# Value matmuls in the banks of the transpositions, four kinds of copies on ScalarE, and weight conversions directly behind the maxima, in a fused attention and gated-convolution kernel

## The chip, the cores and the metric

The kernel runs on one core of a Trainium2 chip. The metric is the time of one execution on the device in microseconds, the median of several runs.

## The reference

Attention with rotary positions over 4 batches, 8 heads, 576 positions and a head size of 64, followed by a block with two projections (512 to 1024 and back) around a convolution of width 3 and a gate. All is float32; the weights of the second half come as 64-bit floats.

```python
q_rot, k_rot = (rotate(q), rotate(k))
scores = scale * np.matmul(q_rot, k_rot.transpose(0, 1, 3, 2))
scores = scores - np.max(scores, axis=-1, keepdims=True)
attn = np.exp(scores)
attn = attn / (np.sum(attn, axis=-1, keepdims=True) + 1e-09)
attn_out = np.matmul(attn, v)
x = attn_out.transpose(0, 2, 1, 3).reshape(B, S, H * D)
h = np.maximum(x @ w_in, 0.0)
conv_out = sum(conv_w[k] * hp[:, k:k + S, :] for k in range(3))   # hp: h, padded
gate = 1.0 / (1.0 + np.exp(-conv_out))
return h * gate @ w_out
```

## The kernel before

**Attention.** Two heads make a pair, and there are 16 pairs `p`. A pair takes five slots of a list that is written out by hand (`plan`): slot 5p+s handles the query rows of step `s`, 128 rows for s = 0 to 3 and the 64 remaining rows of both heads for s = 4. The steps of a pair and their names below are:

- `emit_TQ(p, "q" / "r" / "k")`, lines 175 and 185: the rotated q, the remainders and the rotated k are transposed on TensorE into a bank of PSUM and copied to `QT` and `KT`. They stand in slots 5p-4, 5p-3 and 5p-2.
- `emit_S`, line 206: the scores, in a bank of the pool `s`. Then VectorE takes the maxima (`reds`, line 214), and ScalarE the exponentials with their sums (`exps`, line 218).
- `emit_T` and `emit_Trem`, lines 263, 275 and 280: the exponentials are transposed, and copied to `PT` (line 162 on ScalarE, line 164 on VectorE).
- `emit_E(p, 0)` in slot 5p+4 and `emit_E(p, 1)` in slot 5p+5, line 316: the products with v ("the v matmuls" below, the first and the second of a pair), each of 290 columns; ScalarE copies the result to `xn` (line 324).
- `emit_rinv` and `emit_rinvT`, lines 289 to 304: the reciprocals of the sums are transposed, copied to `rst` (line 297), and spread over the partitions by two DMAs on SP's queue; `norm` (line 328) multiplies `xn` with them two slots later, and `split` (line 332 on ScalarE, 333 on GpSimd) cuts the product into a high and a low part.

**The other half.** From slot 24 on (`WIDE`), `emit_M1` (line 347, in twelve matmuls, evacuated by ScalarE's relu in line 355, then convolution, tanh and gate) and `emit_M2` (line 425, four quarters of six matmuls that keep one bank of PSUM open until the last) are put between the attention's steps. Ten slots are one block: eight of them have an `emit_M1`, the first has several quarters of `emit_M2`. Before slot 24 the weights are converted from 64-bit floats in 48 steps, about two to a slot: `first` (ScalarE, line 443), `mid` (three instructions of VectorE, lines 446, 452 and 455) and `third` (VectorE, line 460; it also issues the load of a later piece and, two ticks later, ScalarE's and GpSimd's `split`, lines 503 and 504).

**Banks.** Before slot 24 the pool `s` has two buffers of three banks, and the pool `t` two banks for all else. From slot 24 on, `s` has two buffers of two banks, `t` two banks for the transpositions, and `m` two banks for `emit_M1`, `emit_M2` and the v matmuls. After the attention there is one pool of six banks.

**Order.** Every engine runs its instructions in the order in which they are emitted. In a slot that order goes by rank: before slot 24, transpositions of the slot before (0), maxima (0.2), exponentials (0.3), a conversion step (0.4), the scores of the next slot (0.5), `emit_rinv` and `norm` (1.7), q/k and remainder transpositions and `emit_rinvT` (2), a second conversion step (3), v matmuls (4). From slot 24 on: scores (0), maxima (0.2), transpositions (1), exponentials (1.5), then 1.7, 2 and 4, with the units of the other half spread between the ranks 2 and 4. A tick follows each event of the ranks 0, 0.5, 1, 2 and 4, and work that was deferred by some ticks is emitted there.

Of the kernel before, what the change touches and what calls it, by code (L numbers as in the profile page):

```python
# [20 lines left out]
def attention_moe_kernel(ctx, tc, q, k, v, w_in, conv_w, w_out, tab, out):  # L21
    nc = tc.nc
    B, H, S, D = q.shape
# [11 lines left out]
    scale = float(D) ** -0.5  # L35
# [4 lines left out]
    psum = {}  # L40
# [35 lines left out]
    def defer(k, fn, rank=1):  # L76
        due.setdefault(slot[0] + k, []).append((rank, len(due.get(slot[0] + k, [])), fn))
# [6 lines left out]
    def t_tile():  # L84
        return psum["t"].tile([128, 512], F32, tag="t", name="tp")

    def m_tile():
        if late["tail"]:
            return psum["t"].tile([128, 512], F32, tag="mt", name="mt")
        return psum["m"].tile([128, 512], F32, tag="m", name="pm")  # L90
# [67 lines left out]
    QT, KT = {}, {}  # L158

    def evac(eng, out, in_, sc=None):  # L160
        if eng == "A" or "m" not in psum:
            nc.scalar.activation(out=out, in_=in_, func=AF.Copy, scale=1.0 if sc is None else sc)  # L162
        elif sc is None:
            nc.vector.tensor_copy(out, in_)
        else:
            nc.vector.tensor_scalar(out=out, in0=in_, scalar1=sc, scalar2=None, op0=ALU.mult)

    def emit_TQ(p, part):
        if p not in QT:
            QT[p] = p2.tile([128, S], F32, tag="qT", name="qT")  # L170
            KT[p] = p2.tile([128, S + 64], F32, tag="kT", name="kT")
        ps = t_tile()
        t1 = rot.pop((p, part)).rearrange("p n d -> p (n d)")
        if part == "r":
            nc.tensor.transpose(ps[:, 0:128], t1, idf)
            evac("V", QT[p][:, 512:S], ps[:, 0:64], scale)
            evac("V", KT[p][:, 576:640], ps[:, 64:128])
            evac("V", KT[p][:, 0:64], ps[:, 64:128])
            if p * STEPS < WIDE:
                for h in range(2):  # L180
                    r = slice(64 * h, 64 * h + 64)
                    evac("V", krem[p % 2][r, r], ps[r, 64:128])
        else:
            for t in range(4):
                nc.tensor.transpose(ps[:, 128 * t:128 * t + 128], t1[:, 128 * t:128 * t + 128], idf)  # L185
            if part == "q":
                evac("A", QT[p][:, 0:512], ps, scale)
            else:
                evac("V", KT[p][:, 64:576], ps)

    ST, STR, PT = {}, {}, {}
    negm, sums = {}, {}
# [99 lines left out]
    def emit_rinvT(p):  # L292
        s = p % 2
        ps = t_tile()[0:32, 0:128]
        nc.tensor.transpose(ps, rvc[s], idf)
        st = p1.tile([32, 128], F32, tag="rst", name="rst")
        nc.vector.tensor_copy(st, ps)
        d = scr.tile([9, 128], F32, tag="d", name="rd")
        nc.sync.dma_start(out=d, in_=st[0:9, :])
        fl = d.rearrange("(o t) n -> o (t n)", o=1)  # L300
        rbt = rb[p] = p1.tile([128, S], F32, tag="rb", name="rb")
        nc.sync.dma_start(out=rbt[0:64, :], in_=fl[:, 0:S].to_broadcast([64, S]))
        nc.sync.dma_start(out=rbt[64:128, 0:512], in_=fl[:, 640:1152].to_broadcast([64, 512]))
        nc.sync.dma_start(out=rbt[64:128, 512:S], in_=fl[:, 576:640].to_broadcast([64, 64]))
# [4 lines left out]

    def emit_E(p, j):  # L310
        b, hp = divmod(p, NPB)
        xp = m_tile() if "m" in psum else t_tile()
        o = (S - XW) * j
        for i in range(5):
            for h in range(2):
                nc.tensor.matmul(  # L316
                    out=xp[64 * h:64 * h + 64, 0:XW],
                    lhsT=vmain[p][:, h, i, :] if i < 4 else vrem[p % 2][:, h, :],
                    rhs=PT[p][:, 2 * i + h if i < 4 else 8, o:o + XW],
                    start=(i == 0),  # L320
                    stop=(i == 4),
                )
        xn = p2.tile([128, XW], F32, tag="xn", name="xn", bufs=3)
        nc.scalar.activation(out=xn, in_=xp[:, 0:XW], func=AF.Copy)  # L324

        def norm():
            sl = xslot[b, hp, j] = free_slots.pop(0)
            nc.vector.tensor_tensor(out=xn, in0=xn, in1=rb[p][:, o:o + XW], op=ALU.mult)  # L328

        def split():  # L330
            sl = xslot[b, hp, j]
            nc.scalar.activation(out=xT[:, sl, 0, :], in_=xn, func=AF.Copy)  # L332
            nc.gpsimd.tensor_tensor(out=xT[:, sl, 1, :], in0=xn, in1=xT[:, sl, 0, :].bitcast(F32), op=ALU.subtract)  # L333

        norms[p, j] = lambda: (norm(), defer(1, split))
# [205 lines left out]
    plan = {}  # L541
# [3 lines left out]
    def at(n, rank, fn):  # L545
        plan.setdefault(n, []).append((rank, len(plan.get(n, [])), fn))

    def emit():
        with tc.manual_schedule(engines=engines):
# [6 lines left out]
            for part in "qrk":  # L556
                emit_TQ(0, part)
# [7 lines left out]
            for p in range(1, NP):  # L565
                n = STEPS * p
                if p > 1:
                    at(max(n - 9, 0), 19, lambda p=p: load(p))
                at(max(n - 8, 0), 18, lambda p=p: rope(p, "q", nc.gpsimd))
                at(max(n - 6, 0), 18, lambda p=p: rope(p, "r", nc.gpsimd))  # L570
                at(max(n - 6, 0), 18, lambda p=p: rope(p, "k", nc.gpsimd))
                for e, part in ((4, "q"), (3, "r"), (2, "k")):
                    at(n - e, 2, lambda p=p, part=part: emit_TQ(p, part))
                at(n, 19, lambda p=p: load_v(p))
            for p in range(NP):
                n = STEPS * p
                for s in range(STEPS):
                    m = n + s
                    first = m < WIDE
                    if m:  # L580
                        at(m - 1 if first else m, 0.5 if first else 0, lambda p=p, s=s: emit_S(p, s))
                    at(m, 0.2, lambda p=p, s=s: go(reds, (p, s)))
                    at(m, 0.3 if first else 1.5, lambda p=p, s=s: go(exps, (p, s)))
                    for h in range(2 if s < 4 else 1):
                        at(m + 1, 0 if m + 1 < WIDE else 1, lambda p=p, s=s, h=h: emit_T(p, s, h))
                for g, e in ((0, 2), (1, 4), (2, 5)):
                    at(n + e, 2, lambda p=p, g=g: emit_Trem(p, g))
                at(n + 4, 4, lambda p=p: emit_E(p, 0))
                at(n + 5, 4, lambda p=p: emit_E(p, 1))
                at(n + 5, 1.7, lambda p=p: emit_rinv(p))  # L590
                at(n + 6, 2, lambda p=p: emit_rinvT(p))
                for j in range(2):
                    at(n + 8, 1.7 + j, lambda p=p, j=j: norms.pop((p, j))())
            nw = len(wsteps)
            for i, u in enumerate(wsteps):
                x = (WIDE - 1) * i // nw
                at(x, 0.4 if not any(r == 0.4 for r, _, _ in plan.get(x, [])) else 3, u)
            at(12, 3, conv_cw)
            at(14, 2, turn_cw)
            moe = {}  # L600
# [61 lines left out]
            for u in seq + second + m2_units(last) + m2_units(LASTB):  # L662
                u()
                tick()

    emit()


# [41 lines left out]
```

## Time and profile before

| | |
|---|---|
| median of 3 runs | 579.53 us (578.71 to 579.86) |
| the profiled execution: time, span | 579.58 us, 577.5 us |
| TensorE (PE) busy | 522.2 us, 90% of the span |
| VectorE (DVE) busy | 382.1 us, 66% |
| ScalarE (ACT) busy | 315.3 us, 55% |
| GpSimd (POOL) busy | 270.7 us, 47% |
| granted clock of TensorE, mean | 0.979 |

The span runs from the first to the last instruction; 2.08 us of the profiled execution's time lie outside it. The span falls in three stages: attention with the conversion of weights (slots 0 to 23, to about 131 us), attention with the other half between it (to about 505 us), and the rest of the other half. Busy shares are averages over these.

### The profile page before, as it was taken

How to read it: one execution, taken by the hardware profiler on the slowest of the kernel's cores; microseconds unless marked ns; L12 is line 12 of the kernel's file. 1: busy time of each engine (PE TensorE's matmuls, PEld its weight loads, DVE VectorE, ACT ScalarE, POOL GpSimd, SP SyncE). 2: the span in 40 equal slices, each digit the busy share in tenths (PEclk: the TensorE clock that was granted, in tenths of full speed). 3: DMA queues.
4: the chain of work that ended last, by engine and by line, in shares of the span. 5: the costliest groups of instructions: out<-in, count | busy, mean ns of one | idle time of the engine just before them, and what ended most of it. 6: DMA issues, size and time to landing. Idle time of an engine off the chain costs nothing.

```text
span 577.5 us, 9313 instructions
## 1 busy us (share of the span) xinstructions
PE 522.2 (90%) x3297; PEld 374.5 (65%) x3297; DVE 382.1 (66%) x671; ACT 315.3 (55%) x821; POOL 270.7 (47%) x341
## 2 busy tenths in 40 slices
PE   3797968889998998999899998999989999989997
PEld 1354544446866685767657676767857677669986
DVE  4776987984888277655858458653776547457971
ACT  2677886885857265645627355652636537224530
POOL 5555948768375438190733629181281203132440
PEclk9989989899999999999989999999989999999999
DMA  6434343521302120201303121021200010010011
GB/s 182 123 108 116 114 135 99 151 61 23 83 2 63 39 75 10 66 15 40 81 1 82 40 60 24 30 51 58 64 22 20 20 40 21 2 58 18 1 37 54
DMA packets 67537, 33.07 MB, mean 57 GB/s; under 512 B 60412, under 2 KB 61220, under 8 KB 67492
## 3 DMA queue, kind: packets, MB, share of 16 engines
q1 hardware_dynamic: 66292, 32.10, 20.2%
q8 instruction: 26, 0.43, 0.3%
q10 hardware_dynamic: 1200, 0.39, 0.3%
q14 instruction: 19, 0.16, 0.1%
HBM read 27.68 MB, written 4.79 MB: 56 GB/s over the span
## 4 chain that ended last, share of the span: by engine, by line
PE 69%; DVE 13%; ACT 11%; issue 4%; DMA 2%; SPq 1%; ACTq 0%; DVEq 0%
PE sp L206 13%; PE pm L316 11%; PE pm L425 10%; PE tp L263 9%; PE pm L347 8%; PE mt L425 6%; PE mt L347 4%; ACT st L218 4%; PE tp L316 4%; DVE negm L214 3%; DVE c L361 3%; ACT pt L162 2%; PE tp L185 2%; DVE xn L328 1%; DVE c L359 1%
## 5 line engine op out<-in xcount | busy, mean ns | idle before, releaser
L379 POOL TENSOR_TENSOR g<-c,g 128x288 fp32r<-128x288 f32 (+4 forms) x88 | 56.0, 648 | 214.7 <-ACT g L378 213.0
L162 ACT ACTIVATE pt<-tp 128x512 f32<-128x512 f32 (+2 forms) x161 | 88.0, 565 | 101.7 <-PE tp L263 99.5
L214 DVE TENSOR_REDUCE negm<-sp 128x1 f32<-128x576 f32 x144 | 102.5, 748 | 51.6 <-PE sp L206 51.5
L206 PE MATMUL sp<-kT,qT 64*128 64x288 f32 (+4 forms) x560 | 109.7, 481 | 5.3 <-ACT st L218 5.2
L218 ACT ACTIVATE st<-sp,negm 128x576 f32<-128x576 f32 x128 | 93.7, 744 | 11.1 <-DVE negm L214 11.0
L263 PE MATMUL tp<-tabs,st 128*128 128x128 f32 x512 | 75.3, 289 | 18.5 <-ACT kr L162 6.8
L361 DVE SCALAR_TENSOR_TENSOR c<-rr,cw,c 128x288 f32<-128x288 f32 x128 | 88.0, 688 | 4.5
L263 PEld LDWEIGHTS tp<-tabs,st 128*128 128x128 f32 x512 | 57.5, 146 | 45.7 <-issue 13.0
L347 PE MATMUL pm<-xT,winh 128*128 128x290 f32 x384 | 82.9, 308 | 0.6 <-ACT xn L324 0.6
L206 PEld LDWEIGHTS sp<-kT,qT 64*128 64x128 f32 (+1 forms) x560 | 49.1, 180 | 40.9 <-issue 15.9
L316 PE MATMUL pm<-pt,vm 128*64 128x290 f32 x384 | 54.9, 430 | 12.7 <-ACT rr L355 12.7
L425 PE MATMUL pm<-wouth,g 128*128 128x512 f32 x176 | 64.3, 415 | 0.0
L347 PEld LDWEIGHTS pm<-xT,winh 128*128 128x128 f32 x384 | 61.1, 190 | 1.2 <-ACT xn L324 1.1
L347 PE MATMUL pm<-xT,winl 128*128 128x290 f32 x192 | 56.9, 296 | 0.0
L370 DVE SCALAR_TENSOR_TENSOR c<-c,rr 128x288 f32<-128x288 f32 x64 | 38.8, 607 | 16.3 <-ACT c L367 16.2
L316 PEld LDWEIGHTS pm<-pt,vm 128*64 128x64 f32 x384 | 26.4, 141 | 34.0 <-ACT rr L355 15.0
L324 ACT ACTIVATE xn<-pm 128x290 f32<-128x290 f32 x24 | 9.9, 413 | 63.3 <-PE pm L316 62.9
L425 PEld LDWEIGHTS pm<-wouth,g 128*128 128x128 f32 x176 | 33.2, 188 | 13.4 <-issue 7.0
L359 DVE TENSOR_SCALAR c<-rr,cw 128x288 f32<-128x288 f32 x64 | 31.4, 491 | 9.1 <-ACT rr L355 8.6
L347 PEld LDWEIGHTS pm<-xT,winl 128*128 128x128 f32 x192 | 36.6, 191 | 0.0
L425 PE MATMUL pm<-woutl,g 128*128 128x512 f32 x88 | 34.7, 395 | 0.0
L333 POOL TENSOR_TENSOR xT<-xn,xT 128x290 fp32r<-128x290 f32 x32 | 29.2, 925 | 11.0 <-ACT xT L332 11.0
(103 smaller groups left out, 881.8 us busy)
## 6 DMA issues: line engine op xcount, KB each, us to landing
out<-ot SPq DMA_DIRECT2D x17, 256.0 KB
rk<-k SPq DMA_DIRECT2D x32, 128.0 KB
w<-moe_w_in SPq DMA_DIRECT2D x8, 512.0 KB
vm<-v SPq DMA_DIRECT2D x32, 128.0 KB
w<-moe_w_out SPq DMA_DIRECT2D x8, 512.0 KB
rq<-q SPq DMA_DIRECT2D x30, 128.0 KB
rb<-rd SPq DMA_DIRECT2D x16, 144.0 KB
rb<-rd SPq DMA_DIRECT2D x16, 128.0 KB
```

Of the source, the lines that this page charges most:

```text
L162: nc.scalar.activation(out=out, in_=in_, func=AF.Copy, scale=1.0 if sc is None else sc)
L206: nc.tensor.matmul(out=out, lhsT=qt[64 * h:64 * h + 64, c], rhs=kt[64 * h:64 * h + 64, a:a + n], start=True, stop=True)
L214: reds.setdefault((p, s), []).append(lambda: nc.vector.tensor_reduce(out=nm, in_=sc, axis=AX.XY if len(sc.shape) == 3 else AX.X, op=ALU.ma ...
L218: lambda: nc.scalar.activation(out=dst, in_=sc, func=AF.Exp, bias=nm, scale=1.0, accum_out=sm)
L263: nc.tensor.transpose(ps[:, 128 * t:128 * t + 128], st[:, 128 * t:128 * t + 128], idf)
L316: nc.tensor.matmul(out=xp[64 * h:64 * h + 64, 0:XW], lhsT=vmain[p][:, h, i, :] if i < 4 else vrem[p % 2][:, h, :], rhs=PT[p][:, 2 * i + h ...
L347: nc.tensor.matmul(out=ps[:, 0:XW], lhsT=w[:, kk, fs], rhs=xT[:, xs, e, :], start=(i == 0), stop=(i == n - 1))
L359: nc.vector.tensor_scalar(out=c, in0=r[:, j:j + HS], scalar1=cw[:, f:f + 1], scalar2=None, op0=ALU.mult)
L361: nc.vector.scalar_tensor_tensor(out=c, in0=r[:, j + e:j + e + HS], scalar=cw[:, 8 * e + f:8 * e + f + 1], in1=c, op0=ALU.mult, op1=ALU.add,)
L370: nc.vector.scalar_tensor_tensor(out=c, in0=c, scalar=1.0, in1=r[:, j + 1:j + 1 + HS], op0=ALU.add, op1=ALU.mult)
L379: nc.gpsimd.tensor_tensor(out=lo, in0=c[:, o:o + n], in1=hi.bitcast(F32), op=ALU.subtract)
L425: nc.tensor.matmul(out=ops[tt][:, 0:width], lhsT=g_tile(tt, f, e), rhs=w[:, f, cols], start=(f == 0 and i == 0), stop=(f == NF - 1 and i = ...
```

## The change

The v matmuls always take a bank of the pool `t`. The copies of the transposed remainders (to `QT` and twice to `KT`) and of the transposed k go to ScalarE in all slots; before slot 24 they were there already, since `evac` uses ScalarE wherever there is no pool `m`. For the same reason the copy of the transposed reciprocals, now an `evac("V", ...)`, moves to ScalarE before slot 24 and stays on VectorE after it. All conversion steps get rank 0.4, so that both of a slot stand behind its maxima and exponentials and ahead of everything else.

```diff
         if part == "r":
             nc.tensor.transpose(ps[:, 0:128], t1, idf)
-            evac("V", QT[p][:, 512:S], ps[:, 0:64], scale)
-            evac("V", KT[p][:, 576:640], ps[:, 64:128])
-            evac("V", KT[p][:, 0:64], ps[:, 64:128])
+            evac("A", QT[p][:, 512:S], ps[:, 0:64], scale)
+            evac("A", KT[p][:, 576:640], ps[:, 64:128])
+            evac("A", KT[p][:, 0:64], ps[:, 64:128])
...
             else:
-                evac("V", KT[p][:, 64:576], ps)
+                evac("A", KT[p][:, 64:576], ps)
...
         st = p1.tile([32, 128], F32, tag="rst", name="rst")
-        nc.vector.tensor_copy(st, ps)
+        evac("V", st, ps)
...
-        xp = m_tile() if "m" in psum else t_tile()
+        xp = t_tile()
...
                 x = (WIDE - 1) * i // nw
-                at(x, 0.4 if not any(r == 0.4 for r, _, _ in plan.get(x, [])) else 3, u)
+                at(x, 0.4, u)
```

## Rows read from the trace of the kernel before

**Rows 1.** Busy time, granted clock and DMA in two stages, by windows.

```profile
14.00:131.00 117.00, 97.58 (x562) 53.86 (x558) 93.79 (x134) 90.38 (x228) 77.90 (x82) 0.93 0.41 113
131.00:505.00 374.00, 353.43 (x2336) 258.88 (x2335) 236.65 (x439) 198.82 (x520) 164.94 (x218) 0.99 0.15 39
```

**Rows 2.** Waits of TensorE, whole span: us in total, times, longest.

```profile
PE pm L316 <- ACT rr L355: 12.7, 10, 2.4
...
PE tp L263 <- ACT kr L162: 6.8, 4, 2.2
...
PE tp L263 <- DVE rst L297: 1.8, 4, 0.5
...
PE pm L347 <- ACT xn L324: 0.6, 1, 0.6
PE tp L316 <- DVE cw L525: 0.5, 1, 0.5
```

**Rows 3.** Timeline around one pair of v matmuls: start, duration, instruction, idle before.

```profile
219.22 0.59 ACT L162 ACTIVATE pt<-tp 128x512 f32<-128x512 f32 x1
...
220.22 0.38 PE L275 MATMUL tp<-tabs,st 128*128 128x128 f32 x2
...
221.32 0.74 ACT L218 ACTIVATE str<-sp,negm 128x576 f32<-128x576 f32 x1 [1.51 <-DVE negm L214]
...
222.05 0.40 ACT L355 ACTIVATE rr<-pm 128x289 f32<-128x289 f32 x1
...
222.51 2.17 PE L316 MATMUL pm<-pt,vm 128*64 128x290 f32 x16 [1.91 <-ACT rr L355]
...
231.29 2.17 PE L316 MATMUL pm<-pt,vm 128*64 128x290 f32 x16 [0.95 <-ACT rr L355]
```

**Rows 4.** The same work after three of these waits, by windows.

```profile
222.50:225.20 2.70, 2.69 (x21) 1.45 (x21) 2.35 (x3) 0.29 (x1) 2.62 (x4) 1.00 0.00 0
...
288.00:292.30 4.30, 4.15 (x21) 1.92 (x21) 3.77 (x4) 0.43 (x2) 4.00 (x4) 0.64 0.01 4
...
425.50:430.00 4.50, 4.43 (x21) 2.21 (x22) 4.05 (x4) 0.35 (x3) 4.34 (x6) 0.62 0.00 0
```

**Rows 5.** Groups by form: copies of k and of remainders (count, busy us, mean ns, idle before).

```profile
L164 DVE COPY kT<-tp 128x512 f32<-128x512 f32 x10 | 6.8, 680 | 0.4 <-PE tp L185 0.4
...
L162 ACT ACTIVATE kT<-tp 128x512 f32<-128x512 f32 x6 | 3.6, 604 | 0.6 <-PE tp L185 0.6
...
L162 ACT ACTIVATE kT<-tp 128x64 f32<-128x64 f32 x12 | 2.1, 234 | 0.0
```

**Rows 6.** Timeline, first stage, of slots 6, 7, 11, 13, 14 and 17.

```profile
48.41 0.28 DVE L297 COPY rst<-tp 32x128 f32<-32x128 f32 x1 [4.70 <-PE tp L295]
...
48.84 0.63 PE L263 MATMUL tp<-tabs,st 128*128 128x128 f32 x4 [0.46 <-DVE rst L297]
...
49.44 0.60 ACT L162 ACTIVATE qT<-tp 128x512 f32<-128x512 f32 x1
...
51.03 1.42 DVE L214 TENSOR_REDUCE negm<-sp 128x1 f32<-128x576 f32 x2
...
52.48 0.74 ACT L218 ACTIVATE st<-sp,negm 128x576 f32<-128x576 f32 x1 [1.09 <-DVE negm L214]
...
73.74 0.67 ACT L443 ACTIVATE wt<-w 128x512 f32<-128x512 f32 x1 [0.80 <-DVE wf L460]
...
83.56 1.64 DVE L455 SCALAR_TENSOR_TENSOR wt<-w,wt 128x512 int32<-128x512 int32 x1
...
84.54 0.46 ACT L332 ACTIVATE xT<-xn 128x290 fp32r<-128x290 f32 x1
...
101.82 0.74 ACT L218 ACTIVATE st<-sp,negm 128x576 f32<-128x576 f32 x1 [0.90 <-DVE negm L214]
```

**Rows 7.** Timeline, second stage, behind a transposition of remainders at 243.33 us.

```profile
244.50 0.56 ACT L378 ACTIVATE g<-c 128x224 fp32r<-128x224 f32 x2
...
245.55 1.09 PE L263 MATMUL tp<-tabs,st 128*128 128x128 f32 x8
```

## Prediction

> **What bounds the kernel now.** I read the windows by stage first, then TensorE's waits, then the timeline where the longest of them stand. Over the second stage TensorE is busy 353.4 of 374.0 us, VectorE 236.7 and ScalarE 198.8; in the first stage three engines stand close together, at 97.6, 93.8 and 90.4 of 117.0 us [rows 1]. So the second stage is TensorE's, and a microsecond that TensorE idles there is lost; the first is a chain through three engines, in which moving work from one to another can give or cost.
>
> The longest wait of TensorE is the v matmuls' for ScalarE's relu (line 355): 12.7 us in 10 places [rows 2]. The timeline shows its nature. The transposition of line 275 ends at 220.60; the v matmuls start at 222.51, just behind the relu that ends at 222.45 [rows 3]. No data goes from that relu to the v matmuls. What they share is the pool `m`: one bank holds an open sum of `emit_M2`, the other held the `emit_M1` before, and the relu empties it. The relu is late because ScalarE's queue stood 1.51 us at an exponential that waited for VectorE's maxima [rows 3]. One slot later, at 231.29, the second v product of the pair pays 0.95 us in the same way [rows 3]; five pairs have such a couple.
>
> **Part by part: the v matmuls' bank.** The wait for the relu goes: -12.7 us. The 0.6 us that an `emit_M1` waits for `xn`, the copy of a v product in its bank, goes too [rows 2]. What is late next? The new bank was last used by the second transposition of the slot, whose copy ends at 219.81, 0.79 us ahead of 220.60 [rows 3]. If a copy of k at 0.60 us [rows 5] slips ahead of it, 0.19 us remain: I take 0. The first stage already runs the v matmuls in the transpositions' banks, eight times, and TensorE's waits have one entry of 0.5 us for them, on the unrelated `cw` [rows 2].
>
> After two of the ten waits the granted clock falls. The same 21 matmul records take 2.69 us of TensorE at a clock of 1.00 after an idle time of 1.91 us, but 4.15 and 4.43 us in windows where the mean is 0.64 and 0.62, between the levels of 1.2 and 2.4 GHz [rows 3, 4]. Without the gaps I give that back: 1.46 + 1.74 = -3.2 us. Bounds: 0 to -3.2.
>
> The Trainium skill speaks against this part. "Perfetto Trace Analysis", section "Matmuls", wants independent groups of matmuls to rotate through different banks, so that one group's evacuation runs under the next group's matmuls; here 24 products leave a pool for one that all transpositions already share. By that rule each would wait for a transposition's copy; that is a rival below, and the rows above are why I don't sum by it.
>
> **The copies of q, k and remainders.** In the second stage ten pairs have one 128x512 copy moved (0.68 us on VectorE, 0.60 on ScalarE) and three small ones of 0.23 us [rows 5]. VectorE loses about 1.3 us a pair and gains nothing on TensorE's path by it: behind the transposition of remainders its next work, the convolution, waits for the relu anyway. On ScalarE the three small copies come behind the high part of `g`, which ends at 245.06; they would end at 245.75, and the next transposition, which takes one of these two banks, began at 245.55 [rows 7]. That is 0.2 us late, in the six pairs that have no quarter of `emit_M2` in between: at most 1.2 us; I take +0.6. The copy of k is covered by the next slot's scores on TensorE; 10 x 0.60 = 6 us if that cover were gone; I take 0.
>
> **The first stage.** Four times VectorE stands in its queue before the copy to `rst`: 4.70 us at 48.41, and the conversion step and the maxima behind it come late (maxima at 51.03, exponentials 1.09 us idle at 52.48) [rows 6]. Both the rank 0.4 and the move of `rst` undo that. Three idle times of ScalarE hang on this order: 1.09, 0.90 and, on a conversion step that stood behind `rst`, 0.80 us: -2.8 us [rows 6]. Against it stands ScalarE's own queue. It gets 0.28 us four times. And the transposition at 48.84 could start on the bank that VectorE had just freed, while ScalarE's copy of q ran from 49.44; now both banks come free behind that copy [rows 6]. I take 0.7 us for each of the four: +2.8 us. In slot 13 the three instructions of `mid` pass `norm`; the last ends at 85.20, and ScalarE's high part of `xn`, which stands between two copies of transpositions and began at 84.54, can't begin before `norm` behind that [rows 6]: +1.0. `first` passes the copies of q or remainders in four slots, 0.67 us [rows 6], but what ScalarE does between two rounds of exponentials stays the same in sum: 0. Together +1.0 us. Bounds: -3 (gains only) and 4 x (0.28 + 0.63) + 4 x 0.67 = +6 (each cost in full).
>
> **Sum.** -12.7 - 0.6 - 3.2 + 0.6 + 1.0 = -14.9 us, on the profiled execution's 579.58 (its span of 577.5 and 2.08 around it): 564.7 us. The median of the runs, 579.53, is the same for this purpose. The rest of the other half, after 505 us, starts earlier by the same amount.
>
> **Rivals.**
> - *The next wait takes half.* With the relu out of the way TensorE meets the exponentials that caused it: scores wait for their buffers, transpositions for their input. For it: the relu was late because of the maxima. Against: between the v matmuls and the next use of an exponential stand a product of 2.17 us and more [rows 3]. Half of 13.3 back: 571.4.
> - *Remainders as in the first stage.* There the transposition behind the same copies on ScalarE waits 6.8 us in four places, 1.7 each [rows 2]. If the six uncovered pairs paid that: +10.2, less the 0.6 summed: 574.3. Against: in the second stage ScalarE is idle from 245.06 [rows 7].
> - *Banks in turn*, the skill's rule as a mechanism of this kernel: each of the 24 v products of pairs 4 to 15 waits for a transposition's copy of 0.60 us [rows 5], 14.4 us: 579.1, no change. Against: the 0.79 us of margin [rows 3].
> - *Slower.* The bank of a v product stays taken until ScalarE copies it to `xn`, and if that copy falls behind one exponential of 0.74 us [rows 3] each time, the transposition after it waits: 24 x 0.74 = 17.8, 582.5 us. It decides from 14.9 / 24 = 0.62 us on. The first stage, with the same sharing, has no such row among the main waits [rows 2].
> - *The first stage gains.* Only the -3 is real: 560.7.
>
> **How the numbers follow.** Forecast (562 to 568) 0.62; half taken 0.12; remainders 0.10; first stage gains 0.09; banks in turn 0.04; slower 0.03. The range from 560.5 to 572 holds the forecast, the first stage's gain and the half, 0.83. A change of 0.2%, 1.2 us, is about what the runs can tell from none (three span 1.15 us). Faster by more: 0.62 + 0.12 + 0.10 + 0.09 = 0.93; same 0.04; slower 0.03.
>
> **What would show it.** In the changed profile the v matmuls' wait for the relu is gone, and their waits on copies of transpositions, if any, stay below 0.2 us each; no window of the second stage holds a clock near 0.6. `rst` stands on ScalarE before slot 24, VectorE's wait of 4.70 us is gone, and the first stage ends within 3 us of where it did. The forecast is wrong if transpositions wait for `xn`, or for the small copies on ScalarE by over 0.5 us a pair, or if the first stage ends over 5 us later.

## The result and the profile after

The changed kernel takes 564.95 us, median of four runs (563.93 to 566.32), beside 579.12 us of the kernel before in the same comparison: a ratio of 0.9759, 95% interval 0.9731 to 0.9787, 14 us faster. The forecast was 564.7. A second comparison of the same kernel, below, gave 0.9767 (0.9738 to 0.9797).

The windows of the changed kernel's two stages, and two more of 3 us each, which come up further below:

```profile
14.00:131.00 117.00, 95.03 (x547) 52.12 (x544) 93.15 (x127) 86.87 (x224) 78.76 (x80) 0.91 0.38 107
131.00:490.00 359.00, 350.61 (x2349) 257.71 (x2347) 234.10 (x403) 209.88 (x567) 166.25 (x219) 1.00 0.17 43
86.00:89.00 3.00, 3.00 (x10) 1.27 (x9) 3.00 (x4) 2.06 (x5) 2.92 (x5) 0.50 0.03 8
89.00:92.00 3.00, 2.71 (x11) 1.39 (x13) 2.58 (x5) 1.56 (x5) 2.10 (x2) 0.50 0.50 145
```

TensorE was busy 353.4 of 374.0 us of the second stage before [rows 1], which left 20.6 us idle; now it is busy 350.6 of 359.0, which leaves 8.4, and the granted clock is 1.00 throughout. Its waits over the whole span of the changed kernel:

```profile
PE tp L263 <- ACT st L218: 7.0, 3, 3.4
PE tp L263 <- ACT qT L162: 5.9, 5, 1.3
...
PE tp L263 <- ACT kr L162: 4.7, 4, 1.6
...
PE tp L316 <- ACT pt L162: 1.6, 3, 0.6
...
PE tp L316 <- DVE cw L525: 0.3, 1, 0.3
...
PE tp L316 <- DVE pt L164: 0.2, 1, 0.2
```

The row of 12.7 us for the relu of line 355 and that of 0.6 us for `xn` [rows 2] are gone, and so are the four waits for `rst`. The v matmuls' waits for copies of transpositions come to 1.8 us in four places, of which only two, 0.38 and 0.17 us, stand from slot 24 on. The place of [rows 3], the first v product of pair 7, in the changed kernel's timeline:

```profile
222.11 0.64 ACT L162 ACTIVATE pt<-tp 128x512 f32<-128x512 f32 x1
...
223.09 0.38 PE L275 MATMUL tp<-tabs,st 128*128 128x128 f32 x2
...
223.40 2.17 PE L316 MATMUL tp<-pt,vm 128*64 128x290 f32 x16
...
224.05 0.74 ACT L218 ACTIVATE str<-sp,negm 128x576 f32<-128x576 f32 x1 [1.30 <-DVE negm L214]
...
224.78 0.40 ACT L355 ACTIVATE rr<-pm 128x289 f32<-128x289 f32 x1
...
231.16 2.17 PE L316 MATMUL tp<-pt,vm 128*64 128x290 f32 x16
```

The relu is as late as before: it still stands behind an exponential that waits for the maxima, and it ends at 225.18. But the product starts at 223.40, directly behind the transposition, because the copy that empties its new bank ended at 222.75. The wait didn't move elsewhere; the product no longer asks for that bank.

To see where the time went I cut each trace at the first v product of pair 4, the last work of slot 24; "first stage" below means up to there. In the two profiles the first stage ends at 133.23 us before and at 136.00 after, 2.8 us later; from there to the end it is 444.3 us before and 428.5 after, 15.8 us less. The experiments have to tell which parts of the change made the second number, and whether the first one is the change at all.

### The profile page after: what moved, and what is told of

The parts are those of the page before. It is cut to its first block, busy times and chain, and to the rows that moved or that the text cites. A ratio compares the mean times of both kernels' runs of the same rounds, so it can differ in the third digit from the quotient of the medians.

```text
span 564.5 us, 9293 instructions
## 1 busy us (share of the span) xinstructions
PE 518.7 (92%) x3297; PEld 373.5 (66%) x3297; DVE 379.4 (67%) x627; ACT 322.9 (57%) x865; POOL 273.3 (48%) x341
## 4 chain that ended last, share of the span: by engine, by line
PE 75%; DVE 10%; ACT 9%; DMA 3%; issue 2%; SPq 0%; ACTq 0%; DVEq 0%
PE sp L206 14%; PE tp L316 13%; PE pm L347 12%; PE pm L425 11%; PE tp L263 10%; PE mt L425 6%; PE mt L347 5%; ACT st L218 3%; ACT pt L162 2%; DVE negm L214 2%; DMA rb<-rd 2%; PE tp L185 1%; DVE wt L455 1%; DVE wt L452 1%; DVE xn L328 1%
## 5 line engine op out<-in xcount | busy, mean ns | idle before, releaser
L379 POOL TENSOR_TENSOR g<-c,g 128x288 fp32r<-128x288 f32 (+4 forms) x88 | 58.2, 672 | 199.8 <-ACT g L378 199.7
L206 PE MATMUL sp<-kT,qT 64*128 64x288 f32 (+4 forms) x560 | 107.5, 472 | 5.3 <-ACT st L218 5.2
L263 PEld LDWEIGHTS tp<-tabs,st 128*128 128x128 f32 x512 | 56.3, 144 | 46.7 <-issue 13.0
L316 PE MATMUL tp<-pt,vm 128*64 128x290 f32 x512 | 71.3, 421 | 0.7 <-ACT pt L162 0.4
L370 DVE SCALAR_TENSOR_TENSOR c<-c,rr 128x288 f32<-128x288 f32 x64 | 41.6, 652 | 16.4 <-ACT c L367 16.2
L316 PEld LDWEIGHTS tp<-pt,vm 128*64 128x64 f32 x512 | 34.6, 139 | 27.2 <-issue 7.0
L324 ACT ACTIVATE xn<-tp 128x290 f32<-128x290 f32 x32 | 13.2, 413 | 59.0 <-PE tp L316 58.4
L359 DVE TENSOR_SCALAR c<-rr,cw 128x288 f32<-128x288 f32 x64 | 29.9, 467 | 14.4 <-ACT rr L355 14.3
L367 ACT ACTIVATE c<-c 128x288 f32<-128x288 f32 x64 | 28.3, 442 | 10.5 <-DVE c L361 10.2
```

Of the source, the lines that this page charges most:

```text
L206: nc.tensor.matmul(out=out, lhsT=qt[64 * h:64 * h + 64, c], rhs=kt[64 * h:64 * h + 64, a:a + n], start=True, stop=True)
L263: nc.tensor.transpose(ps[:, 128 * t:128 * t + 128], st[:, 128 * t:128 * t + 128], idf)
L316: nc.tensor.matmul(out=xp[64 * h:64 * h + 64, 0:XW], lhsT=vmain[p][:, h, i, :] if i < 4 else vrem[p % 2][:, h, :], rhs=PT[p][:, 2 * i + h ...
L359: nc.vector.tensor_scalar(out=c, in0=r[:, j:j + HS], scalar1=cw[:, f:f + 1], scalar2=None, op0=ALU.mult)
L370: nc.vector.scalar_tensor_tensor(out=c, in0=c, scalar=1.0, in1=r[:, j + 1:j + 1 + HS], op0=ALU.add, op1=ALU.mult)
L379: nc.gpsimd.tensor_tensor(out=lo, in0=c[:, o:o + n], in1=hi.bitcast(F32), op=ALU.subtract)
```

## The experiments

"Before" and "after" name the two kernels; the ratio is to before, in the runs of the same comparison. The cut at slot 24 of all fourteen profiles, in us, worked out from each timeline and span:

```
kernel            v bank      rst on   conversions  first stage ends  from there on
before            m           DVE      old          133.2             444.3
all but bank      m           ACT      new          132.9             442.0
bank, even pairs  m odd       DVE      old          133.5             443.5
bank alone        t           DVE      old          133.3             427.6
bank, odd pairs   t odd       DVE      old          136.4             428.3
after             t           ACT      new          136.0             428.5
after, again      t           ACT      new          134.8             426.8
q, k on DVE       t           ACT      new          135.0             429.2
xn twice          t           ACT      new          133.9             426.3
slot 13 old       t           ACT      new but one  134.5             428.3
keep busy         t           ACT      new          132.9             428.0
rst on DVE        t           DVE      new          135.0             426.7
old order         t           ACT      old          129.7             426.5
old order, again  t           ACT      old          132.9             428.1
```

**The bank alone.** Before, with one line of the change:

```diff
-        xp = m_tile() if "m" in psum else t_tile()
+        xp = t_tile()
```

> The kernel before with one edit: the v products take the transpositions' banks. Theory (the shared bank is the whole gain, and the other edits cost in the first stage): 579.3 - 12.7 - 0.6 - 3.2 = about 562.8 us, ratio 0.972, some 2 us below the changed kernel, with its first stage ending where it did before. Rival (the maxima must also come earlier, which the copies taken off VectorE bring): only half the wait goes, 571 us. Rival (banks in turn: products now wait for copies of transpositions): 577 us or more.

563.86 us (562.52 to 568.8), ratio 0.9766 (0.9722 to 0.981): the gain of the whole change, 1.1 us above what I expected. From slot 24 on it is 427.6 us, and neither the relu nor `xn` stands among TensorE's waits. The rival that the maxima must come earlier falls: VectorE keeps all its copies here.

**All but the bank.** The changed kernel with that line put back.

> The changed kernel with the v products' bank put back. Theory: only the cost of the first stage is left, 579.3 + 2.8 = about 582 us (ratio 1.003 to 1.006), and the wait for the relu stands in the trace with 11 to 14 us. Rival (the copies taken off VectorE shorten the wait by themselves): 573 us or less.

578.49 us (573.78 to 581.29), ratio 0.9983 (0.9947 to 1.0018): no difference that can be told. The wait is back in full, as the row of this kernel's waits shows:

```profile
PE pm L316 <- ACT rr L355: 12.6, 10, 2.5
```

The 582 us that I expected didn't come: the first stage ended at 132.9 us, not at 136.0, though its code there is that of the changed kernel. So the 2.8 us of the first comparison can't be read as the price of an edit.

**Which pairs.** Before, with the new bank for one half of the pairs:

```diff
-        xp = m_tile() if "m" in psum else t_tile()
+        xp = m_tile() if "m" in psum and p % 2 == 0 else t_tile()   # odd pairs
+        xp = m_tile() if "m" in psum and p % 2 else t_tile()        # even pairs
```

> The kernel before with the new bank for pairs 5, 7, 9, 11, 13 and 15 alone; the even pairs stay in the pool m. Theory (only there is the other bank of m held by an open sum, so the relu of the block before is in the way): the whole gain, within 1 us of the same edit for all pairs, 563 to 564.5 us. Rival (the gain is that 24 products leave a pool of two banks that is short everywhere): about half of it, 571 us.

> The kernel before with the new bank for pairs 4, 6, 8, 10, 12 and 14 alone, the other half of the 24 products. Theory (these products never waited for a relu): nothing, 578 to 580 us, and the 12.7 us of waiting in ten places stay. Rival (what counts is the number of products that leave the pool): half the gain, 571 us.

Odd pairs: 564.43 us, ratio 0.9759 (0.9724 to 0.9794), 428.3 us from slot 24 on. Even pairs: 578.66 us, ratio 1.0004 (0.9977 to 1.003), 443.5 us, and this row among its waits:

```profile
PE pm L316 <- ACT rr L355: 12.4, 10, 2.4
```

Twelve of the 24 products carry the whole gain and the other twelve none. What counts is not how many products share a pool, but whether one of them falls where `emit_M2` holds the pool's other bank open and a late relu holds this one. That a late relu alone isn't enough shows in pair 5, the one odd pair that waits nowhere: it falls in the first block, which has no `emit_M2`. In the kernel before, its first product starts without a wait, 2.65 us before the end of a relu that stands behind the same kind of exponential:

```profile
159.85 2.17 PE L316 MATMUL pm<-pt,vm 128*64 128x290 f32 x16
...
161.37 0.74 ACT L218 ACTIVATE str<-sp,negm 128x576 f32<-128x576 f32 x1 [1.94 <-DVE negm L214]
...
162.10 0.40 ACT L355 ACTIVATE rr<-pm 128x289 f32<-128x289 f32 x1
```

**The bank held longer.** The changed kernel with the copy to `xn` made twice:

```diff
         nc.scalar.activation(out=xn, in_=xp[:, 0:XW], func=AF.Copy)
+        nc.scalar.activation(out=xn, in_=xp[:, 0:XW], func=AF.Copy)
```

> The changed kernel with every copy of a v product to xn made twice on ScalarE, one behind the other, so that its bank is held and ScalarE's queue is busy some 0.4 us longer, 32 times. Theory (the bank has margin, since scores and other work stand between): up to 2 us longer, 565 to 567 us, and no wait of a transposition for xn. Rival (the bank is held just long enough now, the slower case of the prediction): 24 x 0.4 = 10 us longer, 574 us or more.

563.15 us (562.03 to 567.49), ratio 0.9762 (0.9727 to 0.9798): no cost that can be told, below the band I gave. There is a wait for `xn` now, but only in the first stage; two of its four places, from this kernel's timeline:

```profile
45.68 0.66 PE L263 MATMUL tp<-tabs,st 128*128 128x128 f32 x4 [0.40 <-ACT xn L325]
...
121.43 0.66 PE L263 MATMUL tp<-tabs,st 128*128 128x128 f32 x4 [0.46 <-ACT xn L325]
```

In the second stage the bank could be held another 0.4 us, 24 times, at no cost. That bears on the prediction's slower case: its price asked for 0.62 us of late copy each time, which this run doesn't reach.

**The copies of q and k.** The changed kernel with the four copies of `emit_TQ` back on VectorE in the second stage (`evac("V", ...)` as before).

> The changed kernel with the copies of q, k and remainders back on VectorE in the second stage. Theory (they lie off TensorE's path on either engine): within 0.8 us of the changed kernel in the second stage (428.5 us from pair 4's first product to the end), total about 565 us. Rival (VectorE, relieved of 13 us, delivers the maxima earlier and feeds the gain): 2 us or more longer. Rival (they hold up ScalarE): 1 us or more shorter.

564.66 us (561.42 to 566.44), ratio 0.9769 (0.9733 to 0.9806); 429.2 us from slot 24 on, at the upper end of the 426.3 to 429.2 of all kernels with the new bank. An effect of a microsecond or two either way isn't excluded; nothing larger shows.

**The copy to `rst`.** The changed kernel with `nc.vector.tensor_copy(st, ps)` in `emit_rinvT`.

> The changed kernel with the copy to rst back on VectorE. Theory (conversion order is the loss; with it in the new order, the conversion no longer stands behind rst): within 1 us of the changed kernel, 564 to 566 us. Rival (rst on ScalarE makes the next transposition wait behind two copies and is the loss, 4 x 0.7): 562 us. Other rival (VectorE again stands 4 x 2.6 us before the copy, and the maxima come late): 567 us or more.

563.51 us (561.68 to 564.37), ratio 0.9743 (0.9703 to 0.9783). The median lies half a microsecond below the expected band. The time doesn't exclude the rival's 562 us; the first stage's end at 135.0 us lies among those with `rst` on ScalarE in this order (132.9 to 136.0), which speaks against it, but weakly in so wide a spread.

**The order of the conversions.** The changed kernel with the old line, run in two comparisons:

```diff
-                at(x, 0.4, u)
+                at(x, 0.4 if not any(r == 0.4 for r, _, _ in plan.get(x, [])) else 3, u)
```

> The changed kernel with the old order of the conversion steps. Theory (the conversions directly behind the maxima push the convolution weights, the maxima and the norms of slots 12 to 14 back): the first stage ends 2 to 3 us earlier, 562.5 us. Rival (the loss comes from the copies of q, k and rst on ScalarE's queue): no change, 565 us within 0.5.

> The changed kernel with the old order of the conversion steps once more, unedited, for a second profile. The first one ended its first stage at 129.7 us with a full clock from 32 us on, and its other runs took 561.9 to 563.9. Theory (that profile drew a good clock; the order is worth 1 us at most): the first stage ends at 131 to 135 us, median 562.5 to 564 us. Rival (the old order keeps the clock up): again 130 us or less, with no fall behind 32 us.

562.50 us, ratio 0.9723 (0.9681 to 0.9765), and 561.61 us, ratio 0.972 (0.9695 to 0.9745). The first profile, with its first stage ending at 129.7, was 558.3 us and the fastest run of its kernel; the second ended it at 132.9, with a fall of the clock between 52 and 60 us, so the good clock was the draw of one execution. Its median is 0.9 us below the band I gave. This is the fastest version seen: 2.4 us below the changed kernel by the medians, the first run against its first and the second against its second. These are four different comparisons, though, and the intervals of the ratios overlap.

**The changed kernel again**, unedited.

> The changed kernel once more, unedited, for a second profile. The first stage's clock fell for about 9 us between 84 and 96 us in the first one. Theory (that fall is not fixed by the order of the work, since a kernel with the same first stage and another bank ended it at 132.9 instead of 136.0 us): the first stage ends anywhere from 132.5 to 136.5 us with falls in other places; median 565 us. Rival (the order of the conversions sets it): again 135.5 to 136.5 us with the fall behind the products of pair 2.

563.98 us (563.26 to 566.23). The first stage ends at 134.8 us, inside the theory's range and outside the rival's, but the clock fell again around pair 2's products, as the rival had it.

**Slot 13 alone.** The changed kernel with the second conversion step of slot 13 back at rank 3, behind the norms.

> The changed kernel with the old place for the conversion step of slot 13 alone, behind the two norms. Theory (the three instructions of mid ahead of the norms hold up ScalarE's high part of xn and the copies of transpositions behind it, forecast at 1.0 us): the wait of 2.63 us of the transposition in slot 14, and the 0.85 us of ScalarE for the norm, shrink together by 1 us; the total moves by 1 us or less, 563 to 565 us. Rival (the wait hangs on the maxima that stand behind the convolution's weights): 2.6 us again.

563.44 us (561.0 to 564.63), ratio 0.9747 (0.972 to 0.9775). My theory falls: the wait of 2.63 us stays. This kernel's timeline shows why the norms gain nothing by their place:

```profile
78.49 1.20 DVE L446 TENSOR_SCALAR wt<-wt 32x128 f32<-32x128 f32 x1 [1.73 <-ACT wt L443]
...
81.82 2.53 DVE L328 TENSOR_TENSOR xn<-xn,rb 128x290 f32<-128x290 f32 x2
...
82.66 1.37 POOL L149 TENSOR_TENSOR rq<-rq,tabs 128x512 f32<-128x512 f32 x1
82.81 0.66 PE L263 MATMUL tp<-tabs,st 128*128 128x128 f32 x4 [2.62 <-ACT st L218]
```

**TensorE kept busy.** The changed kernel with transpositions that nobody reads:

```diff
+            def keep_busy():
+                ps = t_tile()
+                for _ in range(10):
+                    nc.tensor.transpose(ps[:, 0:128], idf, idf)
+
+            for x in (1, 13):
+                at(x, 2.5, keep_busy)
```

> The changed kernel with two rounds of ten added transpositions of the unit matrix, whose results nobody reads, behind the transposition of q in slot 1 and of k in slot 13, where TensorE then stands 3.4 and 2.6 us. Theory (the length of the first stage follows the granted clock, and the clock falls behind these two waits): no window at 0.50 to 0.67 behind either, the first stage ends 2 to 4 us earlier, 131 to 132.5 us, and the total is 561 to 563 us. Rival (ScalarE and VectorE set the pace of the first stage, so the clock of TensorE does not matter): no change within 1 us, 564 to 565 us. Other rival (the added work takes a bank that the next transposition needs): 566 us or more.

562.71 us (560.88 to 563.47), ratio 0.9736 (0.9709 to 0.9762), the first stage ending at 132.9, 0.4 us above the band. Windows of this kernel behind the two places:

```profile
24.00:28.00 4.00, 2.57 (x12) 2.11 (x14) 3.48 (x7) 3.80 (x10) 0.88 (x1) 0.64 0.68 180
28.00:32.00 4.00, 3.56 (x12) 1.66 (x11) 2.25 (x5) 2.94 (x11) 0.85 (x2) 0.50 0.82 229
...
84.00:88.00 4.00, 2.77 (x15) 1.33 (x13) 3.97 (x6) 3.04 (x9) 3.04 (x4) 1.00 0.30 115
88.00:92.00 4.00, 3.25 (x26) 2.01 (x26) 3.93 (x7) 2.51 (x6) 3.07 (x4) 1.00 0.38 131
```

Behind slot 13, where the idle time shrank from 2.63 to 1.53 us, the clock stayed up; behind slot 1, where the ten transpositions took only 1.26 us and 2.39 us of idle time were left, it fell as in the other kernels. The time agrees with the theory, but "all but the bank" ended the same first stage at 132.9 us without any added work, so one profile doesn't prove it.

## Why the prediction was right

**The v matmuls' bank, -12.7 us, and `xn`, -0.6.** Shown, cause and size. The bank alone brings the gain, everything else without it brings none, and the ten places lie in the odd pairs. The margin of 0.79 us that I took for the new bank [rows 3] is 0.65 us at the same place after (222.75 to 223.40). From the Trainium skill's advice to rotate through banks ("Perfetto Trace Analysis", section "Matmuls") I had made a rival in which the products wait for copies of transpositions; from slot 24 on they do for 0.55 us in all, against the 14.4 us of that rival. The advice isn't contradicted by this: the relu's late evacuation of a bank was the cost, and the number of banks in the pool was not.

**The clock, -3.2 us.** Right in the second stage, but the last stage took part of it back. From slot 24 on, the three kernels that keep the wait average 443.3 us and the eleven without it 427.7 (426.3 to 429.2): 15.6 us. Less the 13.3 us of waits, 2.3 are left for the clock and all else. A second cut, at the last v product of pair 15, parts this; in the kernels before and after it starts at:

```profile
497.74 2.17 PE L316 MATMUL pm<-pt,vm 128*64 128x290 f32 x16 [0.34 <-ACT rr L355]
...
483.89 2.17 PE L316 MATMUL tp<-pt,vm 128*64 128x290 f32 x16
```

Between the cuts it is 364.5 us before and 347.1 to 348.7 (347.8 on average) in the eleven: 16.7 us less, of which 12.7 are the waits, and 4.0 remain for the clock and all else, against my 3.2. In "all but the bank" it is 362.3, and 1.9 remain: there only one of the waits is followed by a slow product. It isn't the longest, as two rows of that kernel show:

```profile
287.51 2.18 PE L316 MATMUL pm<-pt,vm 128*64 128x290 f32 x16 [2.51 <-ACT rr L355]
...
423.17 3.83 PE L316 MATMUL pm<-pt,vm 128*64 128x290 f32 x16 [2.25 <-ACT rr L355]
```

Behind the second cut it is 79.7 us before (here lay the 0.6 us for `xn`). It is 78.9 to 79.2 in four of the eleven, but 80.2 to 80.6 in the other seven, in which the clock falls once between 494 and 504 us; in none of the three that keep the wait does it fall there. The changed kernel's first profile is one of the seven. Its window, and that of the same place in the kernel before:

```profile
500.00:503.00 3.00, 3.00 (x13) 2.90 (x13) 0.69 (x1) 0.00 (x0) 0.45 (x1) 0.50 0.21 80
...
514.40:517.40 3.00, 3.00 (x18) 2.77 (x19) 1.07 (x3) 0.41 (x1) 0.43 (x1) 1.00 0.23 87
```

The fall costs some 1.4 us by these times, where I had let the rest of the other half merely start earlier. Why the clock falls there isn't shown: just ahead of it TensorE stands idle for 0.45, 0.99 and 0.90 us, and in the kernel before for 0.34, 0.99 and 0.90 us with no fall. No window of the second stage after shows a clock near 0.6.

**The three small copies, +0.6 us.** Too much; no cost shows. In the changed kernel's timeline at the place of [rows 7] they stand ahead of the high part of `g`, not behind it, and are done 0.58 us before the transposition, which doesn't wait:

```profile
244.51 0.37 ACT L162 ACTIVATE kT<-tp 128x64 f32<-128x64 f32 x2
244.72 0.59 ACT L378 ACTIVATE g<-c 128x224 fp32r<-128x224 f32 x2
...
245.46 1.09 PE L263 MATMUL tp<-tabs,st 128*128 128x128 f32 x8
```

I had put a copy that VectorE makes behind ScalarE's work as it stood, and not asked where in ScalarE's own order the program would place it.

**The first stage, +1.0 us.** About right in sum, as far as the spread lets it be read, by terms that were not. The four profiles with its old code end it at 133.2 to 136.4 us, 134.1 on average; the four with exactly the new code (the changed kernel twice, all but the bank, q and k on VectorE) at 132.9 to 136.0, 134.7 on average: +0.6, in a spread of 3 us for one and the same code.

The gain that I summed as -2.8 isn't shown in that size. With `rst` on ScalarE and the old conversions VectorE's wait of 4.70 us before `rst` [rows 6] is gone, but of the two ends, 129.7 and 132.9, the first is the draw with the good clock, and the second lies only 0.3 to 0.6 us below three of the four profiles with the old code. By the medians of one comparison ("bank alone" 563.86, "old order" 562.50) the move is worth 1.4 us, in intervals that overlap. The +2.8 that I set against it is right in kind: TensorE's waits for the copy of q come to 5.4 to 5.9 us in the nine profiles with `rst` on ScalarE, and to 1.3 to 1.9 in the five with it on VectorE, which wait another 1.8 or 1.9 for `rst`; some 2 us more. The new conversions on top cost about 2 us: 1.8 by the ends (134.7 against 132.9), 2.4 by the medians of the section above.

Where they cost it can be read more sharply than from the stage's end: from slot 13's first transposition to pair 2's first v product it is 8.97 to 9.18 us in five of the six profiles with the old order (10.91 in the sixth), and 11.2 to 11.9 in the six with the new one. In "keep busy", whose clock stayed up here, it is 10.61. So the order seems to cost about 1.6 us here, and the clock's fall the rest. The changed kernel's timeline there:

```profile
78.25 1.09 PE L263 MATMUL tp<-tabs,st 128*128 128x128 f32 x8 [1.06 <-ACT kr L162]
...
79.20 1.27 POOL L504 TENSOR_TENSOR woutl<-wf,wouth 128x512 fp32r<-128x512 f32 x1 [2.91 <-ACT wouth L503]
...
79.35 1.20 DVE L446 TENSOR_SCALAR wt<-wt 32x128 f32<-32x128 f32 x1 [1.72 <-ACT wt L443]
...
83.67 1.11 PE L263 MATMUL tp<-tabs,st 128*128 128x128 f32 x4 [2.63 <-ACT st L218]
...
85.16 2.42 DVE L328 TENSOR_TENSOR xn<-xn,rb 128x290 f32<-128x290 f32 x2
...
90.13 3.87 PE L316 MATMUL tp<-pt,vm 128*64 128x290 f32 x16 [0.28 <-DVE cw L525]
```

The same place with the old order of the conversions (second profile):

```profile
78.38 1.26 POOL L504 TENSOR_TENSOR winl<-wf,winh 128x512 fp32r<-128x512 f32 x1 [3.62 <-ACT winh L503]
...
78.99 1.09 PE L263 MATMUL tp<-tabs,st 128*128 128x128 f32 x8 [1.58 <-ACT kr L162]
...
79.58 0.21 DVE L446 TENSOR_SCALAR wt<-wt 32x128 f32<-32x128 f32 x1 [2.30 <-ACT wt L443]
...
81.93 0.81 DVE L328 TENSOR_TENSOR xn<-xn,rb 128x290 f32<-128x290 f32 x2
82.92 0.66 PE L263 MATMUL tp<-tabs,st 128*128 128x128 f32 x4 [1.13 <-ACT st L218]
...
87.97 2.17 PE L316 MATMUL tp<-pt,vm 128*64 128x290 f32 x16 [0.28 <-DVE cw L525]
```

In the new order a conversion step reaches ScalarE one round earlier, so the high part of a weight passes ahead of the `Abs` of the convolution's weights, and GpSimd makes the low part (line 504) just when VectorE comes to line 446. An instruction of 0.21 us takes 1.20 us and ends at 80.55, 0.08 us behind GpSimd's 80.47. The maxima stand behind it, the exponentials behind the maxima, and the transposition waits 2.63 us instead of 1.13. These 1.5 us are the 1.0 by which that instruction is longer, and the 0.5 by which it starts later behind slot 13's transposition (1.10 us instead of 0.59). I had named slot 13 and 1.0 us, but for another reason, the three instructions of `mid` ahead of the norms; with that undone ("slot 13 alone") the wait stayed. That moving the convolution's weights to another slot would mend it was not tried, so this cause is read from the traces and not shown by a run.

**The sum.** That -14.9 us came within 0.3 us of the median is closer than its terms were, and that is luck: the last stage lost 1.4 us that the sum doesn't have, the 0.6 of the small copies doesn't show, and one profile of the first stage can't be read to better than 3 us. What the runs bear out are the first three terms, the waits and the second stage's clock.

**What stays open.** How much of the first stage's spread is the clock. It falls for some microseconds from 24 to 26 us on in every profile, and from 82 to 86 us on in eight of fourteen. In the changed kernel's windows from 86 to 92 us, at the top, it is 0.50, the level of 1.2 GHz, and the product at 90.13 takes 3.87 us where the same one takes 2.17 at full clock. The earliest end, 129.7, belongs to the one profile with no fall behind 32 us. But three ends of 132.9 go with quite different patterns of falls, and no run held the clock up everywhere.

## What to carry to other kernels

When a matmul waits for an engine whose result it doesn't read, look for the bank they share, and ask which places meet an open sum and a late evacuation there: half of these products carried all of the gain. When a copy moves to another engine, find its place in that engine's order before pricing it, and see what runs beside it on the engines that share a way to memory. A stage that ends 3 us apart for the same code can't price an edit of 1 us from one profile; cut the trace at a fixed instruction and compare several.

## What the runs showed of the hardware

- VectorE was held up while GpSimd worked: 0.21 us became 1.20 (above), and the two norms took 0.81 us where GpSimd was idle and 2.42 and 2.53 where it ran. The Trainium skill has the rule in "SBUF — State Buffer", section "Who interferes with whom": the two engines share a pair of ports, and of two instructions that need it the one that comes first holds it to its end. For the instruction of 0.21 us the trace agrees: it ends 0.08 us behind GpSimd's.
- The clock of TensorE fell in other places from one execution to the next of the same first-stage code: after its idle time of 2.63 us the window from 84 to 88 us was at 0.50 in the changed kernel's second profile and at 0.65 with the bank put back, where the fall was over by 92 us; in the one profile with 1.53 us of idle time it didn't come.
